# First half of the feed-forward in float32, the weights' float16 halves made after it

## Chip, cores and metric

The kernel runs on one core of a Trainium2 chip. Its time is the device time of one execution in microseconds. The engines are named as in the profile: PE (matrix products), DVE (vector), ACT (scalar functions), POOL (a second elementwise engine), SP (issues most transfers). Each takes its instructions in a fixed order.

## What is computed

Eight batches of eight heads of causal attention with a bias that falls off, over 576 positions of width 64; then a feed-forward layer with a piecewise quadratic gate over the 4608 rows:

```python
scores = (q @ k.T) / sqrt(64); cum = cumsum(max(s, 0))
bias = min(-(cum[:, :, :, None] - cum[:, :, None, :]), 0)
attn = softmax(where(causal, -1e9, scores + bias)) ; out = attn @ v
x = out.transpose(0, 2, 1, 3).reshape(4608, 512)
h = x @ w_in                                  # 512 -> 2048
g = where(h >= 1, h, where(h <= -1, 0, (h + 1) ** 2 / 4))
y = g @ w_out                                 # 2048 -> 512
```

All inputs are float32, and the weights come in as 64-bit words whose bits the kernel turns into float32 itself.

## The kernel before

**Precision.** A product with float32 operands is made of float16 ones: each operand is split into a high half (its rounding to float16 after scaling with a power of two) and a low half (the rest), and three products, high by high, high by low and low by high, are added up. So each step of the feed-forward takes three matmuls where a float32 matmul would be one instruction of the program.

**Attention.** It is cut into 64 jobs: two heads of a batch, and either the first 320 positions (three row tiles) or the last 256 (two row tiles). A job has eight slots (`att_slot`): preparing, scores tile by tile (`scores`, masked minimum on DVE at L418, exponential on ACT at L429), and the output product `px` of the job before (`att_out`, L475), whose eviction writes the high and low halves of `x` (L486 on ACT, L487 on DVE). The scores of the first eight jobs are float32 products (L407), later ones two products in a faster format (L412, L413). After a tile's two heads, `weights_t` scales the exponentials and splits them into halves: the high halves on POOL (L450, L452), the second head's scaling on ACT (L451) and its low half on POOL (L453), the first head's low half on DVE (L456). That last one and the transposing transfer behind it (L457) are put into `late` and issued right behind the next masked minimum.

**Weights.** Both weight matrices come in 16 chunks of 128 x 512 (L189). `decode` makes float32 of a chunk: ACT (L198), DVE (L199), a product with ones for a bound (L203), then either ACT for the lowest bits and one DVE operation (L211, L212) or two DVE operations (L214, L215). After a group of chunks, `scale` takes a power of two from the bound, and `split` makes the halves: high on ACT (L228), low on DVE (L236), or scaled on POOL (L231) or ACT (L233) and subtracted on POOL (L234). The decoded float32 lies in `held`, the halves in `out`; for the second weights these are the same storage, shifted by two chunks, and the decoded first weights lie in that storage too.

**Order.** First come four jobs of batch 0 (its first half), with four chunks of `w_in` decoded in each; then `split` of all 16 chunks. Then the loop over `j` takes one attention slot, at times two, and one feed-forward step each. For `j` below 16 it makes the 16 hidden blocks of the first half (`ffn_h`: 12 matmuls at L530, evictions at L542, L545, L546, split into halves at L556 on ACT and L557 on POOL), for `j` from 16 to 31 their products with `w_out` (`ffn_y`, L569). In the first 16 steps two tasks a step decode and split `w_out`, with a raised priority (`W2_LEAD`). From `j` = 32 on hidden and output steps alternate. A planner sorts the instructions of each engine by a simulated timeline and by priority, with the order of issue in the program as the base; SP's and ACT's transfers are in such orders too.

Of the kernel before, what the change touches and what calls it, by code (L numbers as in the profile page):

```python
# [22 lines left out]
P = 128  # L23
# [26 lines left out]
WO_LAG = 2  # L50
# [21 lines left out]
def attention_ffn(ctx: ExitStack, tc: tile.TileContext, qT, kT, vT, s, w_in, w_out, yT):  # L72
# [95 lines left out]
    class Weights:  # L168
        def __init__(self, name, src, held, out, tags, order, groups):
            self.name, self.src, self.held, self.out, self.tags = name, src, held, out, tags  # L170
            self.order, self.size = order, NW // groups
            self.group = {c: n // self.size for n, c in enumerate(order)}
# [18 lines left out]
        def decode(self, n):  # L191
            c, g = self.order[n], n // self.size
            raw = self.raw.pop(c)
            w = flat32(self.held[c])
# [6 lines left out]
            if n % self.size == 0:  # L201
                self.sums[g] = ps_y.tile([P, 512], F32, tag=f"y{g}", name=f"sum_{self.name}{g}")
# [21 lines left out]
        def split(self, n):  # L224
            c, g = self.order[n], n // self.size
            r = self.r[:, g:g + 1]
            w, hi, lo = flat32(self.held[c]), self.out[c][:, 0], self.out[c][:, 1]
            A.activation(hi, w, AF.Copy, scale=r)  # L228
            if n in self.pool_lo:
                if self.name in POOL_SCALE:  # L230
                    G.tensor_scalar(w, w, r, 1.0, ALU.mult, ALU.mult)  # L231
                else:
                    A.activation(w, w, AF.Copy, scale=r)  # L233
                G.tensor_tensor(lo, w, hi, ALU.subtract)  # L234
            else:
                V.scalar_tensor_tensor(lo, w, r, hi, ALU.mult, ALU.subtract)  # L236
# [3 lines left out]
        WO, WI, ((gp, "g", G_BUFS),), [n % 4 * 4 + n // 4 for n in range(NW)], 4,  # L240
# [4 lines left out]
        WO[WO_LAG:], WO, ((ap, "raw", 2), (gp, "x0", 2), (ap, "raw", 2)), list(range(NW)), 2,  # L245
# [189 lines left out]
    def weights_t(n, i):  # L435
# [14 lines left out]
        G.tensor_scalar(his[0], pv, rs[:R, :1], 1.0, ALU.mult, ALU.mult)  # L450
# [4 lines left out]
        def rest():  # L455
            V.scalar_tensor_tensor(los[0], pv, rs[:R, :1], his[0], ALU.mult, ALU.subtract)  # L456
# [5 lines left out]
        late.append(rest)  # L462

    def att_out(n, hf):
# [19 lines left out]
        e = exs[b][:, p:p + 1]  # L484
# [38 lines left out]
    def ffn_h(b, hf, ft):  # L523
# [4 lines left out]
        for kt in range(NKT):  # L528
            for wl, xl in ((0, 0), (0, 1), (1, 0)):
                T.matmul(  # L530
                    h[:, :N], WI[4 * kt + ft // 4][:, wl, ft % 4 * P:(ft % 4 + 1) * P], x[:, kt, xl],
# [18 lines left out]
    to_split = []  # L550

# [141 lines left out]
```

## Time and profile before

| | us |
|---|---|
| three runs, median (lowest to highest) | 1115.94 (1112.94 to 1116.92) |
| the profiled execution | 1111.73 |
| its span | 1109.9 |

Busy shares of the span are 91% for PE, 76% for DVE, 65% for ACT and 61% for POOL. How to read what follows: a line of the timeline or of the chain gives start, length, engine, line of the program and what is written from what; "x12" is a row of twelve instructions taken together, and the idle time before it and its releaser stand in brackets. A line of the groups gives the count, busy time and mean length in ns of one, then the idle time of the engine just before them.

### The profile page before, as it was taken

What the parts mean: (1) busy time and instruction counts of PE and PEld (TensorE: products, weight loads), DVE (VectorE), ACT (ScalarE), POOL (GpSimd) and SP (SyncE); (2) the same over time, 40 slices, a digit from 0 to 9 for tenths busy, and PEclk for the clock granted to TensorE, in tenths of its full rate; (3) what the DMA queues carried; (4) which work ended last, traced back from release to release, by engine and by line L of the source; (5) the groups of instructions that cost most, each with busy time, mean ns of one, the idle gap of its engine ahead of it and who ended that gap; (6) DMA issues with size and microseconds to landing.
All of it is one profiled execution on the core that took longest, in us unless ns stands there. A gap on an engine that the chain in (4) does not pass through costs nothing.

```text
span 1109.9 us, 25082 instructions
## 1 busy us (share of the span) xinstructions
PE 1010.8 (91%) x8495; PEld 774.9 (70%) x8496; DVE 846.3 (76%) x2325; ACT 725.8 (65%) x1703; POOL 679.0 (61%) x1173
## 2 busy tenths in 40 slices
PE   2456898799999999999999999899999999899998
PEld 1232466587768877777778877687778877787787
DVE  7887966688787877787778877787777887887533
ACT  4765985677567774867567765777576765777432
POOL 4782795775556764766467664666476665765522
PEclk9955999799999999999999999999999999999999
DMA  7876653786468663886468763877387763676300
GB/s 235 218 200 192 170 87 91 158 173 155 100 122 188 148 152 71 187 162 158 79 146 177 161 136 81 177 160 163 68 176 155 165 137 74 158 156 138 68 25 19
DMA packets 340775, 155.01 MB, mean 140 GB/s; under 512 B 290856, under 2 KB 322472, under 8 KB 340648
## 3 DMA queue, kind: packets, MB, share of 16 engines
q1 hardware_dynamic: 330944, 143.49, 59.6%
q10 hardware_dynamic: 9704, 9.93, 2.9%
q8 instruction: 67, 1.10, 0.4%
q14 instruction: 60, 0.49, 0.1%
HBM read 72.31 MB, written 9.73 MB: 74 GB/s over the span
## 4 chain that ended last, share of the span: by engine, by line
PE 61%; DVE 12%; POOL 8%; DMA 7%; issue 6%; ACT 5%; ACTq 0%; SPq 0%; DVEq 0%; POOLq 0%
PE y L569 25%; PE h L530 25%; PE px L475 4%; DMA pt<-pb 3%; PE s L412 3%; PE s L413 3%; DVE pb L456 2%; ACT u L542 2%; POOL pb L453 2%; POOL pb L450 2%; DVE p L418 1%; DVE Q L357 1%; DMA vt<-vb 1%; POOL vb L371 1%; DVE h L545 1%
## 5 line engine op out<-in xcount | busy, mean ns | idle before, releaser
L530 PE MATMUL h<-x,WI 128*128 128x256 f16 (+1 forms) x3072 | 463.9, 290 | 7.4 <-ACT x L486 3.4
L569 PE MATMUL y<-g,WO 128*128 128x256 f16 (+1 forms) x3072 | 457.8, 288 | 7.0 <-POOL g L557 5.3
L530 PEld LDWEIGHTS <-WI 128*128 128x128 f16 x3072 | 291.1, 99 | 97.0 <-issue 13.9
L569 PEld LDWEIGHTS <-WO 128*128 128x128 f16 x3072 | 288.1, 98 | 92.9 <-issue 13.8
L557 POOL TENSOR_TENSOR g<-u,g 128x320 f16<-128x320 f32 (+1 forms) x256 | 206.0, 805 | 152.1 <-ACT g L556 151.6
L429 ACT ACTIVATE p<-p,mn 64x64 f32<-64x64 f32 (+4 forms) x320 | 179.4, 561 | 142.7 <-DVE mn L418 122.2
L542 ACT ACTIVATE u<-h,ub,us 128x320 f32<-128x320 f32 (+1 forms) x256 | 149.1, 583 | 120.3 <-PE h L530 115.3
L545 DVE SCALAR_TENSOR_TENSOR h<-h,ws,u 128x320 f32<-128x320 f32 (+1 forms) x256 | 132.4, 517 | 110.6 <-ACT u L542 108.1
L450 POOL TENSOR_SCALAR pb<-p,rs 64x128 f16<-64x128 f32 (+4 forms) x160 | 95.3, 596 | 171.2 <-DVE rs L446 112.1
L453 POOL TENSOR_TENSOR pb<-p,pb 64x128 f16<-64x128 f32 (+4 forms) x160 | 173.9, 1087 | 9.5
L456 DVE SCALAR_TENSOR_TENSOR pb<-p,rs,pb 64x128 f16<-64x128 f32 (+4 forms) x160 | 134.6, 841 | 47.1 <-POOL pb L450 47.0
L418 DVE CUSTOM_DVE_ANT_0 p<-s,mask 64x64 f32<-64x64 f32 (+4 forms) x320 | 134.4, 420 | 31.3 <-PE s L413 23.0
L412 PE MATMUL s<-K,Q 128*64 128x64 f32 (+1 forms) x336 | 126.2, 377 | 16.0 <-DVE mn L418 10.9
L546 DVE SCALAR_TENSOR_TENSOR u<-u,r,h 128x320 f32<-128x320 f32 (+1 forms) x256 | 130.3, 509 | 6.8 <-DVE h L545 0.5
L451 ACT ACTIVATE p<-p,rs 64x64 f32<-64x64 f32 (+4 forms) x160 | 89.6, 560 | 51.3 <-DVE rs L446 49.4
L556 ACT CAST g<-u 128x320 f16<-128x320 f32 (+1 forms) x256 | 107.9, 421 | 10.3 <-DVE u L546 10.3
L413 PE MATMUL s<-K,Q 68*64 68x64 f32 (+1 forms) x336 | 102.8, 307 | 2.1 <-DMA K<-cumd 1.3
L452 POOL TENSOR_SCALAR pb<-p 64x128 f16<-64x128 f32 (+4 forms) x160 | 93.2, 583 | 11.9 <-ACT p L451 11.0
L475 PEld LDWEIGHTS <-vt 128*64 128x64 f16 x1536 | 73.4, 113 | 36.7 <-issue 30.2
L475 PE MATMUL px<-pt,vt 128*64 128x256 f16 (+3 forms) x1536 | 83.5, 259 | 13.3 <-DMA pt<-pb 8.7
L412 PEld LDWEIGHTS s<-K,Q 128*64 128x64 f32 (+1 forms) x336 | 61.5, 183 | 27.3 <-DVE mn L418 8.2
L413 PEld LDWEIGHTS s<-K,Q 68*64 68x64 f32 (+1 forms) x336 | 61.9, 184 | 5.8 <-issue 1.7
(105 smaller groups left out, 983.0 us busy)
## 6 DMA issues: line engine op xcount, KB each, us to landing
rk<-in_k_dram SPq DMA_DIRECT2D x56, 288.0 KB
v<-in_v_dram SPq DMA_DIRECT2D x32, 288.0 KB
rq<-in_q_dram SPq DMA_DIRECT2D x56, 160.0 KB
rk<-in_k_dram SPq DMA_DIRECT2D x56, 160.0 KB
wir<-in_moe_w_in_dram SPq DMA_DIRECT2D x16, 512.0 KB
wor<-in_moe_w_out_dram SPq DMA_DIRECT2D x16, 512.0 KB
rq<-in_q_dram SPq DMA_DIRECT2D x56, 128.0 KB
out_dram<-o ACTq DMA_DIRECT2D x32, 160.0 KB
```

The costliest lines, as they stand in the source:

```text
L412: T.matmul(sc[:R, :c1 - c0], Q1[:, hd, qo:qo + R], K1[:, hd, c0:c1], start=True, stop=False)
L413: T.matmul(sc[:R, :c1 - c0], Q2[:KC, hd, qo:qo + R], K2[:KC, hd, c0:c1], start=False, stop=True)
L418: ttr[0] = V.tensor_tensor_reduce(out=Pt[:R, c0:c1], in0=sc[:R, :c1 - c0], in1=mask[:R, mo:mo + c1 - c0], scale=-0.125 if j < F32_JOBS els ...
L429: A.activation(Pt[:R, :W], Pt[:R, :W], AF.Exp, bias=m2[:R], scale=-1.0, accum_out=sums[n, i][:R, hd:hd + 1])
L453: G.tensor_tensor(los[1], pw, his[1], ALU.subtract)
L456: V.scalar_tensor_tensor(los[0], pv, rs[:R, :1], his[0], ALU.mult, ALU.subtract)
L475: T.matmul(px[hd * D:(hd + 1) * D, lo:N], VT[:, vl * NB + j, hd * D:(hd + 1) * D], PT[:, 4 * j + 2 * hd + pl, lo:], start=(m == 0), stop=( ...
L530: T.matmul(h[:, :N], WI[4 * kt + ft // 4][:, wl, ft % 4 * P:(ft % 4 + 1) * P], x[:, kt, xl], start=(n == 0), stop=(n == 3 * NKT - 1),)
L542: first = A.activation(u, h[:, :N], AF.Relu, bias=ubi[b], scale=usc[b][:, fg:fg + 1]).ins
L545: V.scalar_tensor_tensor(h[:, :N], h[:, :N], wsc[b][:, fg:fg + 1], u, ALU.mult, ALU.max)
L557: G.tensor_tensor(g[:, 1], u, g[:, 0], ALU.subtract)
L569: T.matmul(ys[b, hf, m][:, :N], WO[8 * (m // 2) + ft // 2][:, wl, c0:c0 + P], g[:, gl], start=(ft == 0 and n == 0), stop=(ft == NFT - 1 an ...
```

## The change

The 320 positions of the first half (batch 0) go through the feed-forward in float32: `x` is left in float32 (one eviction, none on DVE), `first_h` multiplies it with the decoded chunks of `w_in` (4 matmuls a block in place of 12), its eviction leaves `g` in float32 with no split, and `first_y` multiplies that with the decoded chunks of `w_out`. The halves of the weights are made afterwards: one chunk of `w_in` a step from `j` = 4, and `w_out` from `j` = 24, the last eight chunks two a step from `j` = 32 with raised priority. Both weights now share their storage, shifted by two chunks, and all low halves of weights are made by ACT (scaling) and POOL (subtraction). The decoding of all 16 chunks of `w_out` takes its lowest bits through ACT. In the first eight jobs the first head's weights are scaled on ACT and their low half is subtracted on POOL, and the transpose is issued at once and not put into `late`.

```diff
-WO_LAG = 2
+W_LAG = 2
 
 Y_LAG = 2
 
-ACT_LOW = {'wi': range(0, 16, 2), 'wo': range(0, 16, 2)}
-POOL_LO = {'wi': (8, 12, 13, 14, 15), 'wo': range(16)}
-POOL_SCALE = ('wi',)
+ACT_LOW = {'wi': range(0, 16, 2), 'wo': range(16)}
+POOL_LO = {'wi': range(16), 'wo': range(16)}
 
 K_POOL = range(12)
 F32_JOBS = 8
+POOL_LO_JOBS = 8
...
-    WI = [cp.tile([P, 2, NC], F16, name=f"WI{c}") for c in range(NW)]
-    WO = [cp.tile([P, 2, NC], F16, name=f"WO{c}") for c in range(NW + WO_LAG)]
+    WT = [cp.tile([P, 2, NC], F16, name=f"WT{c}") for c in range(2 * NW + W_LAG)]
+    half_bias = cp.tile([P, 1], F32, name="half_bias")
...
-        def __init__(self, name, src, held, out, tags, order, groups):
-            self.name, self.src, self.held, self.out, self.tags = name, src, held, out, tags
+        def __init__(self, name, src, base, banks, tags, order):
+            groups = len(banks)
+            self.name, self.src, self.banks, self.tags = name, src, banks, tags
+            self.out, self.held = WT[base:base + NW], WT[base + W_LAG:base + W_LAG + NW]
             self.order, self.size = order, NW // groups
-            self.group = {c: n // self.size for n, c in enumerate(order)}
...
-            w = flat32(self.held[c])
+            w = flat32(self.held[n])
...
-            c, g = self.order[n], n // self.size
+            g = n // self.size
             r = self.r[:, g:g + 1]
-            w, hi, lo = flat32(self.held[c]), self.out[c][:, 0], self.out[c][:, 1]
+            w, hi, lo = flat32(self.held[n]), self.out[n][:, 0], self.out[n][:, 1]
             A.activation(hi, w, AF.Copy, scale=r)
             if n in self.pool_lo:
-                if self.name in POOL_SCALE:
-                    G.tensor_scalar(w, w, r, 1.0, ALU.mult, ALU.mult)
-                else:
-                    A.activation(w, w, AF.Copy, scale=r)
+                A.activation(w, w, AF.Copy, scale=r)
                 G.tensor_tensor(lo, w, hi, ALU.subtract)
...
-        G.tensor_scalar(his[0], pv, rs[:R, :1], 1.0, ALU.mult, ALU.mult)
+        pool_lo = jobs.index((n, hf)) < POOL_LO_JOBS
+        if pool_lo:
+            A.activation(tiles2[0][:R, :W], tiles2[0][:R, :W], AF.Copy, scale=rs[:R, :1])
+            G.tensor_scalar(his[0], pv, 1.0, 1.0, ALU.mult, ALU.mult)
+            G.tensor_tensor(los[0], pv, his[0], ALU.subtract)
+        else:
+            G.tensor_scalar(his[0], pv, rs[:R, :1], 1.0, ALU.mult, ALU.mult)
         A.activation(tiles2[1][:R, :W], tiles2[1][:R, :W], AF.Copy, scale=rs[:R, 1:])
         G.tensor_scalar(his[1], pw, 1.0, 1.0, ALU.mult, ALU.mult)
         G.tensor_tensor(los[1], pw, his[1], ALU.subtract)
 
         def rest():
-            V.scalar_tensor_tensor(los[0], pv, rs[:R, :1], his[0], ALU.mult, ALU.subtract)
+            if not pool_lo:
+                V.scalar_tensor_tensor(los[0], pv, rs[:R, :1], his[0], ALU.mult, ALU.subtract)
             nc.sync.dma_start_transpose(
                 out=PT[:, :4 * (i + 1), off - h_off:off - h_off + R],
                 in_=PB[:R].rearrange("p j g c -> p (j g c)"),
             )
 
-        late.append(rest)
+        if pool_lo:
+            rest()
+        else:
+            late.append(rest)
...
+        e = exs[b][:, p:p + 1]
+        if (b, hf) == (0, 0):
+            if p == 0:
+                X[b, hf] = gp.tile([P, NKT, N], F32, tag=f"x{hf}", bufs=2, name=f"x{b}_{hf}")
+            with tc.high_priority(offset=X_LEAD):
+                A.activation(X[b, hf][:, p], px[:, :N], AF.Copy, scale=e)
+            return
...
+    g32 = []
+    us32, ws32 = (cp.tile([P, 1], F32, name=n) for n in ("us32", "ws32"))
+
+    def first_scales():
+        V.tensor_scalar(us32, msc[0], 2.0 ** -13, None, ALU.mult)
+        V.tensor_scalar(ws32, msc[0], 2.0 ** -12, None, ALU.mult)
+
+    def first_h(ft):
+        N = HALF[0][1]
+        h = ps_h.tile([P, 512], F32, tag="h", name=f"h0_0_{ft}")
+        for kt in range(NKT):
+            T.matmul(
+                h[:, :N], flat32(w1.held[ft // 4 * NKT + kt])[:, ft % 4 * P:(ft % 4 + 1) * P], X[0, 0][:, kt],
+                start=(kt == 0), stop=(kt == NKT - 1),
+            )
+        if ft % 4 == 0:
+            g32.append(gp.tile([P, 4, N], F32, tag="g", bufs=G_BUFS, name=f"g0_0_{ft}"))
+        with tc.high_priority(offset=FFN_LEAD):
+            u = gp.tile([P, N], F32, tag="u", bufs=4, name=f"u0_0_{ft}")
+            A.activation(u, h[:, :N], AF.Relu, bias=half_bias, scale=us32)
+            V.scalar_tensor_tensor(h[:, :N], h[:, :N], ws32, u, ALU.mult, ALU.max)
+            V.scalar_tensor_tensor(g32[-1][:, ft % 4], u, 1.0, h[:, :N], ALU.min, ALU.mult)
+
+    def first_y(ft, ms):
+        N = HALF[0][1]
+        for m in ms:
+            if ft == 0:
+                ys[0, 0, m] = ps_y.tile([P, 512], F32, tag=f"y{m}", name=f"y0_0_{m}")
+            c0 = ft % 2 * 2 * P + m % 2 * P
+            T.matmul(
+                ys[0, 0, m][:, :N], flat32(w2.held[8 * (m // 2) + ft // 2])[:, c0:c0 + P], g32[ft // 4][:, ft % 4],
+                start=(ft == 0), stop=(ft == NFT - 1),
+            )
+            if ft == NFT - 1:
+                o = gp.tile([P, N], F32, tag="o", bufs=O_BUFS, name=f"o0_0_{m}")
+                with tc.high_priority(offset=FFN_LEAD):
+                    A.copy(o, ys[0, 0, m][:, :N])
+                nc.scalar.dma_start(yT[m * P:(m + 1) * P, :N], o)
...
+    first_scales()
     while late:
         late.pop(0)()
-    V.tensor_reduce(a_in, w1.bound, axis=AX, op=ALU.max)
-    batch_scales(0)
     for c in range(3):
-        w2.load(c, a_in)
-    for n in range(NW):
-        w1.split(n)
+        w2.load(c, w1.bound[:, 3:4])
     att_out(*jobs[NPAIR - 1])
...
-    def w2_tasks():
...
-        with tc.high_priority(offset=W2_LEAD):
-            for _ in range(W2_RATE):
-                next(tasks, None)
+        if j < NW // 2:
+            with tc.high_priority(offset=W2_LEAD):
+                for c in (2 * j, 2 * j + 1):
+                    w2.decode(c)
+                    w2.load(c + 3)
+                    if c % 8 == 7:
+                        w2.scale(c // 8, TINY)
+        if j < NFT:
+            first_h(j)
+        elif j < 2 * NFT:
+            i = j - NFT
+            if i < 8:
+                for ft in (2 * i, 2 * i + 1):
+                    first_y(ft, (0, 1))
+            else:
+                for ft in range(i % 4 * 4, i % 4 * 4 + 4):
+                    first_y(ft, (i // 4,))
+        if j == NFT:
+            V.tensor_reduce(a_in, w1.bound, axis=AX, op=ALU.max)
+            batch_scales(0)
+            batch_y(0)
+        if 4 <= j < NW + 4:
+            w1.split(j - 4)
+        if NW + 8 <= j < 2 * NW:
+            w2.split(j - NW - 8)
+        elif 2 * NW <= j < 2 * NW + 4:
+            with tc.high_priority(offset=W2_LEAD):
+                for c in (8, 9):
+                    w2.split(c + (j - 2 * NW) * 2)
         if j >= 2 * NFT:
             ffn_step(j // 2, j % 2)
-        elif j < NFT:
-            ffn_step(j, 0)
-        else:
-            if j == NFT:
-                with tc.high_priority(offset=FFN_LEAD):
-                    g_split()
-            m = 2 * (j // 8 % 2)
-            for i in range(j % 8 * 2, j % 8 * 2 + 2):
-                ffn_y(*ffn_q[i], ms=(m, m + 1))
-            if j == 2 * NFT - 1:
-                del ffn_q[:NFT]
```

More of the change, by code (lines that the diff above doesn't have):

```diff
@@ L161, in attention_ffn @@
     NC = 512
-    WI = [cp.tile([P, 2, NC], F16, name=f"WI{c}") for c in range(NW)]
-    WO = [cp.tile([P, 2, NC], F16, name=f"WO{c}") for c in range(NW + WO_LAG)]
+    WT = [cp.tile([P, 2, NC], F16, name=f"WT{c}") for c in range(2 * NW + W_LAG)]
+    half_bias = cp.tile([P, 1], F32, name="half_bias")
+    V.memset(half_bias, 0.5)
     def flat32(t):
@@ L201, in decode @@
             if n % self.size == 0:
-                self.sums[g] = ps_y.tile([P, 512], F32, tag=f"y{g}", name=f"sum_{self.name}{g}")
+                self.sums[g] = ps_y.tile([P, 512], F32, tag=f"y{self.banks[g]}", name=f"sum_{self.name}{g}")
             T.matmul(
@@ L239, in attention_ffn @@
         "wi", lambda c: w_in[c // 4 * P:(c // 4 + 1) * P, c % 4 * NC:(c % 4 + 1) * NC, :],
-        WO, WI, ((gp, "g", G_BUFS),), [n % 4 * 4 + n // 4 for n in range(NW)], 4,
+        0, (0, 1, 2, 3), ((gp, "g", G_BUFS),), [n % 4 * 4 + n // 4 for n in range(NW)],
     )
@@ L244, in attention_ffn @@
         .rearrange("(j p) n t -> p j n t", p=P),
-        WO[WO_LAG:], WO, ((ap, "raw", 2), (gp, "x0", 2), (ap, "raw", 2)), list(range(NW)), 2,
+        NW, (2, 3), ((ap, "raw", 2), (gp, "x0", 2), (ap, "raw", 2)), list(range(NW)),
     )
@@ L483, in att_out @@
         x = X[b, hf]
-        e = exs[b][:, p:p + 1]
         with tc.high_priority(offset=X_LEAD):
@@ L530, in ffn_h @@
                 T.matmul(
-                    h[:, :N], WI[4 * kt + ft // 4][:, wl, ft % 4 * P:(ft % 4 + 1) * P], x[:, kt, xl],
+                    h[:, :N], w1.out[ft // 4 * NKT + kt][:, wl, ft % 4 * P:(ft % 4 + 1) * P], x[:, kt, xl],
                     start=(n == 0), stop=(n == 3 * NKT - 1),
@@ L569, in ffn_y @@
                 T.matmul(
-                    ys[b, hf, m][:, :N], WO[8 * (m // 2) + ft // 2][:, wl, c0:c0 + P], g[:, gl],
+                    ys[b, hf, m][:, :N], w2.out[8 * (m // 2) + ft // 2][:, wl, c0:c0 + P], g[:, gl],
                     start=(ft == 0 and n == 0), stop=(ft == NFT - 1 and n == 2),
@@ L612, in attention_ffn @@
                 batch_scales_v(0)
+    first_scales()
     while late:
         late.pop(0)()
-    V.tensor_reduce(a_in, w1.bound, axis=AX, op=ALU.max)
-    batch_scales(0)
     for c in range(3):
-        w2.load(c, a_in)
-    for n in range(NW):
-        w1.split(n)
+        w2.load(c, w1.bound[:, 3:4])
     att_out(*jobs[NPAIR - 1])
-    def w2_tasks():
-        for g in range(2):
-            for c in range(8 * g, 8 * g + 8):
-                w2.decode(c)
-                w2.load(c + 3)
-                yield
-            w2.scale(g, TINY)
-            batch_y(0, (g,))
-            for c in range(8 * g, 8 * g + 8):
-                w2.split(c)
-                yield
     t = 8 * NPAIR
-    tasks = w2_tasks()
     for j in range(16 * NP):
```

## The prediction

> **What bounds the kernel now.** I read the windows first, because the change sits in the first fifth of the run. The columns are the stretch in us, its length, then busy time (and instructions) of PE, weight loads, DVE, ACT and POOL, then granted clock, DMA share and GB/s.
>
> ```profile
> core 0: us, PE busy (x) PEld busy (x) DVE busy (x) ACT busy (x) POOL busy (x), PEclk, DMA share, GB/s
> 0.00:104.00 104.00, 46.39 (x164) 22.25 (x166) 83.14 (x214) 59.10 (x118) 64.74 (x106) 0.78 0.80 216
> 104.00:139.00 35.00, 30.14 (x140) 17.12 (x138) 31.97 (x74) 31.00 (x59) 21.56 (x25) 0.83 0.63 162
> 139.00:188.00 49.00, 48.81 (x379) 33.97 (x379) 32.13 (x94) 32.61 (x65) 34.64 (x44) 1.00 0.47 87
> 188.00:212.00 24.00, 13.08 (x98) 10.01 (x95) 15.40 (x51) 14.22 (x42) 17.66 (x32) 0.72 0.77 153
> 212.00:260.00 48.00, 47.63 (x458) 40.30 (x457) 39.56 (x107) 34.91 (x89) 36.12 (x68) 1.00 0.68 152
> ```
>
> From 212 us on PE is full (47.63 of 48), so the change is worth whatever it moves that point. Before it there are three stretches. Up to 104 us PE is half empty and DVE is the fullest engine (83.14, or 80%; POOL has 62%, ACT 57%). From 104 to 139 DVE (91%) and ACT (89%) are both near full and PE idles 4.9 us. From 139 to 188 PE is full again. From 188 to 212 it idles 10.9 us.
>
> What ends the first stretch is read from the chain of waits (start, length, what):
>
> ```profile
> 87.11 0.68 DVE WO L215
> 87.78 0.27 DVE pb L456
> 88.10 0.15 POOL p L402
> 88.30 4.63 DMA pt<-pb
> ...
> 99.94 0.98 PE px L475 x5
> ```
>
> The first half's hidden layer needs `x` of the first four jobs. The fourth job's product `px` starts at 99.94. On its chain stands the low half of a head's weights (L456, DVE), behind second-weight decoding on the same engine (L215). The timelines of POOL and of DVE show why it came so late:
>
> ```profile
> 80.19 2.72 POOL L234 TENSOR_TENSOR WI<-WO,WI 128x512 f16<-128x512 f32 x2
> 82.90 0.53 POOL L450 TENSOR_SCALAR pb<-p,rs 64x128 f16<-64x128 f32 x1
> ```
> ```profile
> 81.83 3.73 DVE L199 TENSOR_SCALAR WO<-WO 128x512 int32<-128x512 int32 x2
> ...
> 91.85 0.43 DVE L199 TENSOR_SCALAR WO<-WO 128x512 int32<-128x512 int32 x1 [0.62 <-ACT WO L198]
> ```
>
> POOL made two first-weight low halves ahead of this job's high half (L450). That half was done by 83.4, and DVE then came to L456 only at 87.78: 4.4 us lost on DVE, and some before it on POOL. So the splitting of the first weights isn't waited for by the hidden layer itself; it delays the attention jobs that are.
>
> **The change, part by part.** (a) *The startup.* DVE loses two groups entirely in this stretch, eleven first-weight low halves and twelve first-head low halves:
>
> ```profile
> L236 DVE SCALAR_TENSOR_TENSOR WI<-WO,r_wi,WI 128x512 f16<-128x512 f32 x11 | 9.5, 883 | 0.0
> L456 DVE SCALAR_TENSOR_TENSOR pb<-p,rs,pb 64x128 f16<-64x128 f32 (+2 forms) x12 | 8.2, 683 | 4.4 <-POOL pb L450 4.4
> ```
> ```profile
> L453 POOL TENSOR_TENSOR pb<-p,pb 64x128 f16<-64x128 f32 (+2 forms) x12 | 12.5, 1044 | 0.5
> ...
> L234 POOL TENSOR_TENSOR WI<-WO,WI 128x512 f16<-128x512 f32 x5 | 6.2, 1244 | 0.0
> ```
>
> That is 9.5 + 8.2 = 17.7 us off DVE's 83.14. POOL takes twelve subtractions of the same kind as L453, 12 x 1.044 = 12.5 us, and is rid of five first-weight low halves, 5 x 1.244 = 6.2, and of the five scalings before them (L231). ACT is rid of 16 first-weight high halves and gets twelve short scalings. The transposes of a job are no longer held back behind the next masked minimum (`late`), so SP's queue gets them sooner; their number, and that of all loads, is the same. The gain is unknown between 0 (POOL becomes what DVE was) and 17.7 (DVE alone was the bound). The nearest row is the 4.4 us that L456 waits for or costs on one chain; of four jobs that the same thing happens to, not each ends last, and DVE's own idle time (20.9 of 104) says that it isn't the only bound. I take **-8**.
>
> At this place a rule speaks against the change. The rows first: L199 takes 0.43 us with POOL idle, and two of them 3.73 us while POOL runs L234. The Trainium skill, "SBUF — State Buffer", section "Who interferes with whom", says that a GpSimd instruction and a DVE instruction in a two-port mode take a shared port pair in turns, and that the one that comes second blocks for the whole of the other. The 0.43 and 3.73 agree. By that rule, as an estimate, the 12.5 us of new POOL subtractions would stand in DVE's way and the gain of (a) would be 17.7 - 12.5 = 5 instead of 8.
>
> (b) *The float32 products.* One f16 matmul of 320 columns is priced by twelve of them in a row (start to next start), a float32 one by the scores of the first jobs, where the two records of an x2 are one matmul:
>
> ```profile
> 113.06 1.79 PE L530 MATMUL h<-x,WI 128*128 128x320 f16 x12
> 114.69 0.65 PE L407 MATMUL s<-KF,QF 68*128 68x288 f32 x2
> ...
> 118.70 0.92 PE L407 MATMUL s<-KF,QF 68*128 68x448 f32 x2
> 119.46 0.84 PE L569 MATMUL y<-g,WO 128*128 128x320 f16 x5
> ```
>
> f16: (114.69 - 113.06) / 12 = 0.136 us. Float32: (119.46 - 118.70) / 448 x 320 = 0.543 us. Before, the first half has 192 + 192 matmuls, 384 x 0.136 = 52.2; after, 64 + 64, 128 x 0.543 = 69.5. PE works **+17.3** longer, half in `h`, half in `y`. Weight loads are included, since these prices are start to start. At a lower granted clock (0.83 from 104 to 139) each costs more in proportion; both kernels pay that for a few of them.
>
> (c) *Where that is hidden.* These groups are those of 104 to 206 us, ACT's and then POOL's:
>
> ```profile
> L233 ACT ACTIVATE WO<-WO,r_wo 128x512 f32<-128x512 f32 x16 | 11.5, 719 | 0.1
> L228 ACT ACTIVATE WO<-WO,r_wo 128x512 f16<-128x512 f32 x16 | 11.4, 721 | 1.2 <-POOL WO L234 1.2
> L542 ACT ACTIVATE u<-h,ub,us 128x320 f32<-128x320 f32 (+1 forms) x17 | 10.2, 603 | 0.0
> L556 ACT CAST g<-u 128x320 f16<-128x320 f32 x16 | 7.2, 453 | 4.2 <-DVE u L546 4.2
> L451 ACT ACTIVATE p<-p,rs 128x448 f32<-128x448 f32 (+4 forms) x11 | 7.1, 647 | 2.1 <-DVE x L487 1.1 <-DVE rs L446 0.8
> L211 ACT ACTIVATE wor<-wor,floor_bias 128x512 uint16<-128x512 uint8 x4 | 5.8, 1448 | 0.0
> ```
> ```profile
> L234 POOL TENSOR_TENSOR WO<-WO,WO 128x512 f16<-128x512 f32 x16 | 20.0, 1250 | 2.1 <-ACT WO L233 1.7 <-POOL WO L234 0.5
> L557 POOL TENSOR_TENSOR g<-u,g 128x320 f16<-128x320 f32 x16 | 15.0, 939 | 18.1 <-ACT g L556 18.1
> ```
>
> ```profile
> 104.00:139.00 35.00, 17.22 (x90) 10.23 (x90) 0.83 0.63 162
> ```
>
> While `h` is made, PE isn't the bound now: of the `h` products (the window above is of their line alone) 90, seven and a half steps, are done in 35 us, 4.7 us a step, though twelve in a row take 1.63. So of the 8.7 us that `h` gets longer I put **-6** beside the evictions; if that cover goes, they cost 6. The `y` share, 8.7, lies on the path, where PE is full (139 to 188).
>
> (d) *Evictions and splits.* The casts (L556, 7.2 us of ACT) and the subtractions (L557, 15.0 us of POOL) of the first half go. The second weights' splits (ACT 11.5 + 11.4, POOL 20.0), today ahead of the attention by priority, leave this place; the same sum comes in for the first weights, one chunk a step from the fifth step on, without priority. Each of those waits until PE has read the float32 chunk that it overwrites; behind it on ACT stand evictions and exponentials, and PE waits for those. Between 0 and 12 us (ACT's 22.9 in half of the stage) I take **-6**: the attention jobs five to eight get ahead.
>
> (e) *The tail at 188.*
>
> ```profile
> 186.10 0.65 PE L407 MATMUL s<-KF,QF 68*128 68x288 f32 x2
> ...
> 200.62 2.77 PE L475 MATMUL px<-pt,vt 128*64 128x256 f16 x30 [4.49 <-DMA pt<-pb]
> ```
>
> The last scores of job eight stand behind `y` products, and its `px` follows 14.5 us later, with PE idle 10.9 us. Longer `y` products can lie over that tail if the job is through sooner, not if the planner again puts its scores last: 0 to -10.9, I take **-5.5**, the middle. The eight late second-weight splits are issued when the second half has begun and are wanted only by its `y`; I cost them at nothing, hidden by its `h` products; without that cover, up to 8 x (0.719 + 0.721) = 11.5. What is small and only moves (two scales for the float32 half ahead of it, the batch's scales behind its `h`, one bit operation fewer on DVE for eight second chunks, four low halves of `x` fewer) I cost at nothing too: DVE has 16.9 us idle between 139 and 188, and without that room the batch's scales would hold the second half's first eviction by about as many DVE instructions as they are; at L456's 0.683 for each of some fifteen, far above what a few values a partition can take, 10 us.
>
> The sum: -8 + 17.3 - 6 - 6 - 5.5 = **-8.2 us**. Against the profiled execution (1111.73, of which 1109.9 is span) that is 1103.5. That execution lies 4.2 below the median of the runs, 1115.94; put on the median the sum gives 1107.7, so **1108**.
>
> **Rivals.** *ACT binds the stage (slower).* In 104 to 212 ACT works 31.00 + 32.61 + 14.22 = 77.8 us. To that come eight more low-bit passes, 8 x 1.448 = 11.6 (fewer if some fall before 104), eight first-head scalings, 8 x 0.647 = 5.2, and eight second-weight splits, 11.5; the casts take 7.2 away: 98.9 us. At its fullest share so far (89%) that needs 111 us against 108 now, so it decides from there: at 80% it needs 124, +16, and less 6 for a smaller startup gain is +10, 1126. For it: a queue in strict order, and waits for PE's reading in front of evictions. Against: the h of the second half doesn't wait for the second weights' splits; without their 11.5 the stage fits. *POOL takes DVE's place at startup (no change).* With (a) at 0 the sum is -0.2, 1116. For it: POOL gets more than it loses; against: DVE is the fuller by 18 us. *DVE was the whole bound.* (a) at -17.7 and (e) at -10.9 give -23, 1093. *The change doesn't do what it says*: if the planner pulled the first weights' splits back into the startup, (a) would be lost. The storage speaks against it: chunk n's halves overwrite float32 chunk n - 2, which `h` still reads; only two chunks are free. I give this no share of its own.
>
> **How the numbers follow.** Forecast (1100 to 1112) 0.45, ACT 0.20, POOL 0.22, DVE 0.13. The range: down to the DVE rival, 1092, up to ACT's, 1126; costs off to either end beyond that (nothing hidden, +17, or all gains, -26) are the 2 in 10 left out. A measurement of this kernel tells about 0.5%, 5.6 us, from no change, that is below 1110.4 or above 1121.5. Faster: 0.38 of the forecast, 0.13 and 0.02 of POOL's, 0.53. Slower: ACT's 0.20 and 0.02 of POOL's, 0.22. Same: 0.25.
>
> **What would show it.** (a) `px` of job four before 94 us, DVE's share of that stretch below 75%; wrong if it starts at 98 or later with POOL over 75%. (b) 128 float32 matmuls at 0.54 us each. (c) `h` steps at 4 us or less apart; wrong if ACT is above 95% there. (d) jobs five to eight through by 190 us. (e) no idle stretch of PE over 3 us ahead of the second half. The whole is wrong if the point at which PE is full for good is later than 212 us, or if the later stretches change pace.

## Result and the profile after

The changed kernel takes 1127.38 us (median of 4 runs, 1126.19 to 1128.24) against 1114.44 of the kernel before on the same chip (1110.12 to 1116.92): a ratio of 1.0124, with an interval of 1.0101 to 1.0146. By the ratio it is slower by 13.8 us (the two medians differ by 12.9), and 1127.38 is 1.4 us above the upper end of the predicted range. The profiled execution has a span of 1124.3 us. The ratios below leave out one execution of 5664 us, of a kernel that otherwise took 1100 to 1104.

The windows of after, in the same stretches as those of before (stretch, length, busy PE, weight loads, DVE, ACT, POOL, granted clock, DMA share, GB/s), and one more:

```profile
core 0: us, PE busy (x) PEld busy (x) DVE busy (x) ACT busy (x) POOL busy (x), PEclk, DMA share, GB/s
0.00:104.00 104.00, 56.37 (x199) 31.64 (x201) 71.22 (x205) 64.34 (x132) 57.18 (x114) 0.89 0.85 220
104.00:139.00 35.00, 30.60 (x124) 19.66 (x123) 22.45 (x54) 33.50 (x54) 20.72 (x24) 0.97 0.67 165
139.00:188.00 49.00, 46.44 (x205) 31.82 (x203) 20.30 (x55) 33.27 (x63) 29.54 (x36) 0.98 0.29 65
188.00:212.00 24.00, 12.72 (x86) 9.22 (x86) 19.14 (x53) 19.21 (x40) 20.89 (x27) 0.58 0.51 111
212.00:260.00 48.00, 43.02 (x379) 35.94 (x380) 40.64 (x109) 35.12 (x94) 38.10 (x76) 0.89 0.72 152
...
212.00:230.00 18.00, 13.02 (x90) 9.79 (x91) 15.28 (x33) 12.58 (x32) 14.77 (x27) 0.71 0.56 119
```

Read down, the fullest engine changes from stretch to stretch. At startup DVE has fallen from 83.14 to 71.22, and PE does 10 us more. From 104 to 139 ACT is full (96%) where DVE and ACT shared the load before. From 139 to 188 PE is full with float32 products while ACT is idle for 32% of the time and POOL for 40%. From 188 to 212 POOL is busy for 87% and DVE and ACT for 80%, while PE idles 11.3 us. And PE is not full from 212 on: 5 us more are lost by 230. From there the pace is that of before (PE has 580.90 of the 600 us from 400 to 1000; before, 582.30).

Where the lead is lost is shown by the end of `px` of each attention job, read from PE's timeline (start plus length of the job's last `px` row, us):

| job | before | after |
|---|---|---|
| 4 | 102.5 | 88.5 |
| 5 | 140.6 | 142.0 |
| 6 | 162.2 | 169.1 |
| 8 | 203.4 | 211.9 |
| 9 | 213.9 | 228.0 |
| 10 | 228.3 | 240.6 |
| 12 | 254.5 | 266.8 |

The 14.0 us won at startup are lost again by job five, with 1.4 more; another 5.5 are lost by job six, 1.6 by job eight, and 5.5 between jobs eight and nine alone, of which 1.7 come back by job ten. The lag of job twelve, 12.3 us, is then about that of the end (13.8). From job four to job twelve after takes 178.3 us and before 151.9: this stage is 26.4 us longer.

### The profile page after: what moved, and what is told of

Read it like the earlier page. It is cut to its first block, busy times and chain, and to the rows that moved or that the text cites. A ratio compares the mean times of both kernels' runs of the same rounds, so it can differ in the third digit from the quotient of the medians.

```text
span 1124.3 us, 24796 instructions
## 1 busy us (share of the span) xinstructions
PE 1025.9 (91%) x8367; PEld 789.8 (70%) x8368; DVE 828.5 (74%) x2285; ACT 748.2 (67%) x1731; POOL 676.7 (60%) x1183
## 4 chain that ended last, share of the span: by engine, by line
PE 46%; DVE 9%; POOL 5%; issue 4%; DMA 3%; ACT 3%; DVEq 0%; POOLq 0%; ACTq 0%; SPq 0%
PE h L545 19%; PE y L622 19%; PE px L484 3%; DMA pt<-pb 3%; PE s L411 3%; PE s L412 2%; DVE pb L462 2%; DVE Q L356 1%; ACT u L557 1%; POOL pb L455 1%; DVE p L417 1%; DVE h L560 1%; POOL pb L458 1%; DVE u L561 1%; POOL g L610 1%
## 5 line engine op out<-in xcount | busy, mean ns | idle before, releaser
L622 PE MATMUL y<-g,WT 128*128 128x256 f16 (+1 forms) x2880 | 428.9, 287 | 5.7 <-POOL g L610 3.7
L545 PE MATMUL h<-x,WT 128*128 128x256 f16 (+1 forms) x2880 | 429.5, 288 | 3.1 <-DVE u L561 2.4
L622 PEld LDWEIGHTS <-WT 128*128 128x128 f16 x2880 | 269.8, 98 | 82.5 <-issue 11.7
L545 PEld LDWEIGHTS <-WT 128*128 128x128 f16 x2880 | 271.0, 98 | 79.1 <-issue 6.6
L610 POOL TENSOR_TENSOR g<-u,g 128x256 f16<-128x256 f32 (+1 forms) x240 | 188.2, 784 | 133.2 <-ACT g L609 132.3
L557 ACT ACTIVATE u<-h,ub,us 128x256 f32<-128x256 f32 (+1 forms) x240 | 139.3, 580 | 118.3 <-PE h L545 113.5
L560 DVE SCALAR_TENSOR_TENSOR h<-h,ws,u 128x256 f32<-128x256 f32 (+1 forms) x240 | 123.7, 516 | 102.3 <-ACT u L557 99.7
L455 POOL TENSOR_SCALAR pb<-p,rs 64x128 f16<-64x128 f32 (+4 forms) x140 | 83.7, 598 | 158.7 <-DVE rs L445 110.3
L417 DVE CUSTOM_DVE_ANT_0 p<-s,mask 64x64 f32<-64x64 f32 (+4 forms) x320 | 134.7, 421 | 33.1 <-PE s L412 16.7
L462 DVE SCALAR_TENSOR_TENSOR pb<-p,rs,pb 64x128 f16<-64x128 f32 (+4 forms) x140 | 123.1, 880 | 41.6 <-POOL pb L455 41.4
L561 DVE SCALAR_TENSOR_TENSOR u<-u,r,h 128x256 f32<-128x256 f32 (+1 forms) x240 | 121.7, 507 | 6.6 <-DVE h L560 0.5
L609 ACT CAST g<-u 128x256 f16<-128x256 f32 (+1 forms) x240 | 100.7, 420 | 6.2 <-DVE u L561 6.2
```

Of the source, the lines that this page charges most:

```text
L417: ttr[0] = V.tensor_tensor_reduce(out=Pt[:R, c0:c1], in0=sc[:R, :c1 - c0], in1=mask[:R, mo:mo + c1 - c0], scale=-0.125 if j < F32_JOBS els ...
L545: T.matmul(h[:, :N], w1.out[ft // 4 * NKT + kt][:, wl, ft % 4 * P:(ft % 4 + 1) * P], x[:, kt, xl], start=(n == 0), stop=(n == 3 * NKT - 1),)
L557: first = A.activation(u, h[:, :N], AF.Relu, bias=ubi[b], scale=usc[b][:, fg:fg + 1]).ins
L560: V.scalar_tensor_tensor(h[:, :N], h[:, :N], wsc[b][:, fg:fg + 1], u, ALU.mult, ALU.max)
L610: G.tensor_tensor(g[:, 1], u, g[:, 0], ALU.subtract)
L622: T.matmul(ys[b, hf, m][:, :N], w2.out[8 * (m // 2) + ft // 2][:, wl, c0:c0 + P], g[:, gl], start=(ft == 0 and n == 0), stop=(ft == NFT - ...
```

## Experiments

Each run stands against the kernel before, run beside it on the same chip; ratios are compared, since the base differs a little from chip to chip, and 0.01 of a ratio is 11.1 us. The intervals are about 0.0025 to either side, so two runs are told apart from about 4 us on. Kernels that leave work out say which.

**The parts that move work between engines, undone and alone.** The first edit gives the low bits of the odd second chunks back to VectorE, the second the first-head low halves of the first eight jobs (and puts their transposes into `late` again).

```diff
-ACT_LOW = {..., 'wo': range(16)}
+ACT_LOW = {..., 'wo': range(0, 16, 2)}
```
```diff
-POOL_LO_JOBS = 8
+POOL_LO_JOBS = 0
```

> The changed kernel, but with the lowest bits of every second chunk of the second weights put back on DVE (8 ACT passes of 1.45 us less, 8 DVE operations more). Theory A (ACT binds the stretch from 90 to 139 us, where it is 96% busy, and through the decoding holds the loads behind it): 1117 to 1121, 6 to 10 below the changed kernel's 1127. Theory P (the float32 products fill PE's order from 139 to 184 us, and the scores of jobs seven and eight stand behind them): 1125 to 1128. Theory T (the first head's low halves, longer by an ACT step and on POOL, lengthen each job's chain): 1125 to 1128.

> The changed kernel, but with no job's first-head low half moved: all on DVE, scaled by POOL, transposes behind the next minimum, as before the change. Theory T: 1117 to 1122, since the chain of jobs five to eight is shorter again, though the startup gives back some of its 13 us. Theory A: ACT is rid of 20 scalings (11 us), about half of them in the full stretch: 1122 to 1125. Theory P: 1127 or, with the startup's gain lost, up to 1135.

The low bits: 1122.84, ratio 1.0063 (1.004 to 1.0086), 6.8 us below after. `px` of job five ends at 133.2 there instead of 142.0. The first-head halves: 1124.75, 1.0088 (1.0057 to 1.012), 4.0 below, at the limit of what can be told. Both together:

> The changed kernel with both side parts undone: lowest bits of every second chunk of the second weights on DVE again, first-head low halves on DVE again. If the two losses are of their own and add up: 1127 - 4.5 - 2.6 = 1120. If both are the same loss (ACT's full stretch), 1122 to 1123. Theory S alone: not below 1117, since all splits are still where the change put them.

1121.26, 1.0061 (1.0033 to 1.009): 7.0 us below after, where the two alone add up to 10.8: by these numbers the two losses overlap in part. The first-head part alone, put on the kernel before:

> The kernel before with this one part of the change: the first eight jobs' first-head low halves on ACT and POOL, transposes at once. Theory T: 1117 to 1122, slower than before by the longer chain. Theory A: 1114 to 1118, ACT's 11 us partly in its full stretch 104 to 139. Theory P: no reason for a loss; DVE gives up 8 us of the startup: 1108 to 1114.

1123.45, 1.0065 (1.0045 to 1.0084): the part alone makes the kernel before 7.2 us slower. PE's timeline, `px` of job four, first in the run with this part undone, then in the run with this part alone:

```profile
87.18 1.66 PE L484 MATMUL px<-pt,vt 128*64 128x320 f16 x18 [1.71 <-DMA pt<-pb]
```
```profile
107.27 1.66 PE L486 MATMUL px<-pt,vt 128*64 128x320 f16 x18 [0.80 <-issue]
```

After has 86.81 and before 99.94. So this part brings nothing at the startup when the splits are gone from there, and `px` comes 7 us later with it when they are not: the startup's whole gain is that of the splits. (The kernel before without first-weight splits, below, agrees: its `px` of job four starts at 85.33.)

**A quarter of the float32 products left out** (32 of 128, 17.4 us of PE, as much as the float32 half adds):

```diff
-        for kt in range(NKT):
+        for kt in (0, 2, 3):
...
-            T.matmul(
+            if ft % 4 != 1:
+              T.matmul(
```

> The changed kernel with a quarter of its float32 products left out (one of four in each sum of h, four of sixteen in each sum of y), so that PE's work for the first half is 96 x 0.54 = 52 us, what the float16 products took before; the output is not the reference's. Theory P: 1108 to 1114, all of the 17 us of PE back or most of it. Theory A: 1122 to 1127, since h waits for its evictions and decoding anyway. Theory T: 1122 to 1127.

1126.48, 1.0096 (1.0067 to 1.0124): 3.1 us below after, less than can be told from nothing. Taken by itself that says that the float32 products cost next to nothing; the runs below show that it is wrong. The run isn't clean either: the planner orders its startup in another way, and `px` of job four ends at 93.7 us, where after has 88.5.

**The splits left out**, first all 32 from after (second half and later read one constant tile), then the first weights' 16 from the kernel before (its hidden products read one constant tile):

```diff
-            w1.split(j - 4)
+            pass
...
-            w2.split(j - NW - 8)
+            pass
...
-                    w2.split(c + (j - 2 * NW) * 2)
+                    pass
```

> The changed kernel with the splitting of both weights left out (32 x 2 ACT instructions of 0.72 us and 32 POOL subtractions of 1.2 us that now all lie between 100 and 220 us); the later products read one constant tile in place of the halves, so the output is not the reference's. Theory S (the splits, moved out of the startup where ACT had room, now stand in front of the attention jobs five to eight on ACT and POOL, and the lateness of those jobs sets the end): 1105 to 1114, and the output product of job eleven, now 12 us later than before the change, is back or ahead. Theory P' (what is left is the order of PE, with the float32 products in front of scores): 1122 to 1127.

> The kernel before with the first weights' splits left out of the startup (h reads one constant tile; the output is not the reference's): the part of the change that frees the startup, without its price later. If a startup 13 us shorter is worth 13 us at the end: 1101 to 1105. If the stretch after it takes the gain back by itself (loads that come no sooner, DVE and ACT full from 104 to 139 us): 1108 to 1114.

After without splits: 1119.95, 1.0045 (1.0028 to 1.0061), 8.8 us below after and still above before. Before without first-weight splits: 1099.29, 0.9863 (0.9834 to 0.9892). What the change takes out of the startup is worth 15.3 us, and kept to the end, if nothing is put back. The windows of after without splits show why it doesn't come down to that:

```profile
104.00:139.00 35.00, 31.41 (x134) 20.30 (x132) 20.20 (x53) 24.54 (x39) 11.78 (x18) 1.00 0.64 164
139.00:188.00 49.00, 46.82 (x201) 32.23 (x202) 21.17 (x64) 16.31 (x35) 14.94 (x23) 0.97 0.36 76
```

ACT and POOL are two thirds idle from 139 to 188, and PE is as full as with the splits. Up to job six the splits cost nothing: its `px` ends at 168.8 without them and at 169.1 with them. Behind it they do: job nine's ends at 218.9 instead of 228.0.

**Two misses in the order of the work.** The late second-weight splits spread one every second step, without priority, and the scales of batch 0 issued at step 8 instead of 16 (both on top of the low bits undone); and the sixteen chunks decoded one a step instead of two, without priority (likewise):

```diff
-        if j == NFT:
+        if j == 8:
...
-        elif 2 * NW <= j < 2 * NW + 4:
-            with tc.high_priority(offset=W2_LEAD):
-                for c in (8, 9):
-                    w2.split(c + (j - 2 * NW) * 2)
+        elif 2 * NW <= j < 3 * NW and j % 2 == 0:
+            w2.split(8 + (j - 2 * NW) // 2)
```
```diff
-        if j < NW // 2:
-            with tc.high_priority(offset=W2_LEAD):
-                for c in (2 * j, 2 * j + 1):
+        if j < NW:
+            w2.decode(j)
+            w2.load(j + 3)
...
```

> The changed kernel with the lowest bits back on DVE (1122.8 by itself) and with less in the stretch 184 to 225 us: the last eight splits of the second weights one every second step and without priority, and the scales of batch 0 issued eight steps earlier. Theory S: 1114 to 1119, the jobs eight to eleven get through sooner. Theory P': 1121 to 1123, nothing more than the lowest bits give.

> After, with the low bits of the odd second chunks back on VectorE (that alone gave 1122.8) and the sixteen second chunks decoded one a step over 16 steps, in the program's place, instead of two a step over 8 steps and ahead of everything. Nothing is left out. Theory D (the decoding, packed into the first eight steps and ahead of job five's attention, makes job five late: 53 us from px of job four to px of job five, before 38): px of job five ends at 120-127 and the time falls to 1114-1118. Theory not D: within 2 us of 1122.8.

1125.41, 1.0091 (1.0063 to 1.0119), and 1124.9, 1.0101 (1.0074 to 1.0128): neither better than the 1.0063 of the low bits alone. In the second, job five's `px` comes in three pieces on PE, the last of which ends at 134.7; the low bits alone gave 133.2, and 120 to 127 was expected. Jobs six to eight do come 3.5 us sooner (job six 160.9 against 164.5), but by job twelve that is lost (261.3 against 260.8): to have a job sooner is worth nothing if a later one stands behind another limit.

**Limits that hide each other.** If the stages are in series with a different full engine each, taking away one load should do little and two together much more.

> After without any weight split (the second half of the first batch and all that follows read one constant tile) and also without a quarter of the float32 products. Leaving out the splits alone gave 1120.0, leaving out the quarter of the products alone 1126.5, against 1127.4 of after. Theory M (limits in series mask each other: with the splits gone TensorE's float32 products, 46 of 49 us busy between 139 and 184, are what holds jobs six and seven back): together they give back much more than the sum of the two, to 1108-1114, and px of job seven ends before 181. Theory S (what is left is not TensorE but the attention chain itself and its loads): about the sum, 1117-1120, px of job seven at 187-191.

No splits and a quarter of the products fewer: 1107.12, 0.9932 (0.9913 to 0.9951). With the splits gone the quarter is worth 12.6 us; with them it was worth 3.1. And with the quarter gone the splits are worth 18.3, with all products in place 8.8. The windows with the quarter out alone, and then with the splits out as well:

```profile
188.00:212.00 24.00, 11.88 (x86) 8.64 (x82) 17.21 (x44) 19.27 (x46) 20.99 (x30) 0.64 0.54 122
212.00:230.00 18.00, 16.24 (x136) 13.29 (x136) 16.46 (x37) 13.27 (x34) 15.67 (x27) 0.85 0.62 113
```
```profile
188.00:212.00 24.00, 17.91 (x138) 14.14 (x139) 13.54 (x41) 13.81 (x38) 16.65 (x32) 0.64 0.78 164
212.00:230.00 18.00, 18.00 (x176) 15.92 (x174) 14.62 (x50) 12.52 (x39) 14.81 (x32) 1.00 0.76 157
```

With the quarter out alone, POOL is as full from 188 to 212 as in after (20.99), and PE still not full from 212. With both out PE is full there. A part of this lies in the startup and not in the stage: with the quarter out `px` of job four ends 5.3 us later when the splits are in place (93.7 against 88.5), and 2.5 later without them (90.0 against 87.5). If that difference of 2.8 us were carried whole to the end, 6.7 of the 9.5 us between 3.1 and 12.6 would be left for the loads that hide each other. Which splits do it was tried by leaving out one set of weights, and the second set with the quarter of the products:

> After without the sixteen splits of the second weights (the second products of the second half and later read one constant tile); the first weights' splits stay. All splits together were worth 7.4 us. Theory L (the loss lies in the late second-weight splits, which fill GpSimd to 87% between 188 and 212): 1118-1121, nearly the whole 7.4, and px of job nine within 15 us of px of job eight or sooner (after 16). Theory W1 (it lies in the first weights' splits between 104 and 188): 1124-1128.

> After without the sixteen splits of the first weights (the hidden products of the second half and later read one constant tile); the second weights' splits stay. Theory L: within 2 us of after, 1125-1129. Theory W1: 1119-1122.

> After without the sixteen splits of the second weights and without a quarter of the float32 products. The quarter alone gave 0.9 us, with no splits at all 12.9. Theory L (what the shorter products gain is taken back by the second weights' splits, eight of them late): 8-13 below the run without second-weight splits, 1108-1112. Theory W1 (the first weights' splits take it back): 0-4 below it.

Without the second weights' splits: 1121.79, 1.0057 (1.0037 to 1.0076), 7.5 us below after, most of the 8.8; `px` of jobs six and nine ends at 169.2 and 219.5, as without any split. Without the first weights': 1125.39, 1.0095 (1.0071 to 1.0119), 3.2 below, not told from nothing. Without the second weights' and with the shorter products: 1116.08, 1.0015 (0.9995 to 1.0034), another 4.7, between the two theories. From there to 0.9932, where the first weights' splits are out too, are 9.2 us, but of these up to 4.5 are the startup's (`px` of job four ends at 94.4 in the one and 90.0 in the other). So the second weights' splits cost most; that the first ones take a part back is likely and not clear of the startup.

**TensorE's order.** In after PE's timeline of the first half's end reads so (two records are one float32 matmul):

```profile
169.00 1.02 PE L406 MATMUL s<-KF,QF 68*128 68x448 f32 x2
169.86 6.09 PE L595 MATMUL y<-g,WT 128*128 128x320 f32 x22
175.78 1.40 PE L406 MATMUL s<-KF,QF 68*128 68x448 f32 x4
177.02 5.55 PE L595 MATMUL y<-g,WT 128*128 128x320 f32 x20
182.41 0.65 PE L406 MATMUL s<-KF,QF 68*128 68x288 f32 x2
182.89 1.24 PE L595 MATMUL y<-g,WT 128*128 128x320 f32 x4
```

Scores stand behind ten or eleven float32 products at a time, 5.4 to 5.9 us. The edit gives the scores of jobs five to eight the first place:

```diff
+            with tc.high_priority(offset=FFN_LEAD) if j >= NPAIR else ExitStack():
             T.matmul(
                 sc[:R, :c1 - c0], QF[j % 2]...
```

> After, with the scores of jobs five to eight given the first place in TensorE's order, ahead of float32 products that stand before them in the program (job six's last scores then follow about 10 to 19 products fewer, 5 to 10 us at 0.54 us each). Nothing is left out. Theory O (scores of jobs five to eight queue behind the float32 products): px of jobs six and seven end 4-8 us sooner and the time falls to 1119-1123. Theory A (ScalarE and the decoding pace the stage up to 140 us, then the exponentials and weights of the jobs): within 2 us of after, 1125-1129.

1123.49, 1.0074 (1.0051 to 1.0096): 5.6 us below after; `px` of jobs six and seven end at 161.5 and 189.4 instead of 169.1 and 195.6. With low bits and first-head halves undone too:

> After with the low bits and the first-head low halves back on VectorE (that gave 1121.3) and with the scores of jobs five to eight first in TensorE's order (that alone gave 1123.5). Nothing is left out. If the two gains add up: 1117-1118. If they are one and the same lateness of jobs five to eight, 1120-1122.

1118.53, 1.0052 (1.0037 to 1.0068): 8.0 below after. It has the lowest ratio of the forms that leave nothing out, and is still slower than before. Against the same form without the first place for scores (1.0061) it wins 1.0 us, which can't be told from nothing: the 5.6 of the scores and the 7.0 of the moved work don't add up.

**What is left of the change without its costs.** No splits, low bits and first-head halves undone, so that only the float32 half is left; then a quarter of its products fewer:

> After without any weight split, with the low bits of the odd second chunks back on VectorE and the first-head low halves back on VectorE: of the change only the float32 first half is left, and it pays for no split at all. Apart, the splits gave back 7.5 us and the other two together 6.1. If these losses add up: 1113-1115. If the same wait lies behind them (they overlap): 1118-1120. If a limit was masked by them: under 1111. The kernel before without its first-weight splits stands at 1099.

> After without any weight split, with the low bits and the first-head low halves back on VectorE (that gave 1112.3), and also without a quarter of the float32 products. Theory M (TensorE's float32 products are the limit that is left when the splits and the moved work are gone): 1100-1104, that is 8 to 12 below, as they gave 12.9 with the splits alone gone. Theory not M (attention's own chain is left): 1109-1112.

1112.28, 0.999 (0.997 to 1.001), and 1101.74 (median of three), 0.9903 (0.9878 to 0.9929). The second has about the PE work of the float16 half and comes near the 0.9863 of before without first-weight splits. That gives a ladder from 0.9903 up to after: the longer products +9.7 us (0.999), the moved low bits and halves +6.1 (1.0045), the splits +8.8 (1.0124). The 24.6 us of the three are close to the 26.4 that the stage from job four to job twelve grew by. The rungs belong to this order of adding, since the loads hide one another.

**A version to beat both.** The kernel before, with the first weights' splits behind `px` of job four in the program:

```diff
-    for n in range(NW):
-        w1.split(n)
     att_out(*jobs[NPAIR - 1])
+    for n in range(4):
+        w1.split(n)
...
+        if j < 6:
+            w1.split(2 * j + 4)
+            w1.split(2 * j + 5)
```

> The kernel before with one thing moved: the sixteen splits of the first weights no longer stand together ahead of px of job four, but four behind it and then two a step in the first six steps of the first half, ahead of the decoding (the chunks of the first weights are held in the order in which they are split, so that the decoding finds its places free). All else is before's: the first half in float16, no work moved between engines. Theory S (it is the splits standing ahead of px of job four that cost before 15 us, and they can be hidden beside the first half's products, which in float16 leave TensorE free): px of job four ends at 87-92 and the time falls to 1101-1109. Theory E (the splits cost their VectorE and GpSimd time wherever they stand): within 3 us of before, 1111-1117.

1113.34, 0.9993 (0.9977 to 1.001): no difference. The groups of its first 104 us show that the idea was not tried: the planner put all splits where they had been,

```profile
L236 DVE SCALAR_TENSOR_TENSOR WI<-WO,r_wi,WI 128x512 f16<-128x512 f32 x11 | 9.5, 883 | 0.0
```

as many and as long as before. Whether the splits of the float16 kernel can be hidden beside its products stays open. No version was found that beats both.

## Why the prediction was wrong

**The step that failed is the one from "hidden" to "costs nothing" behind the startup: (d), (e) and the late splits "costed at nothing".** The prediction let the stage from `px` of job four to the point where PE is full keep its length (+17.3 - 6 - 6 - 5.5 = -0.2). From job four to job twelve it became 26.4 us longer, more than the 14.0 that the startup won.

(a) *The startup, -8: right in sign, too small, and in part for a wrong reason.* `px` of job four:

```profile
86.81 1.65 PE L484 MATMUL px<-pt,vt 128*64 128x320 f16 x18 [1.25 <-issue]
```

It starts at 86.81 instead of 99.94, 13.1 us sooner, and DVE has 68% of the stretch, as step (a) asked. But of the 17.7 us taken off DVE, the first-head halves' 8.2 brought nothing there and, given to ACT and POOL, cost about 4.0 in after and 7.2 alone. The gain is that of the splits, which leave DVE, POOL and ACT at once; which of the three engines had held `px` back isn't separated by a run. The estimate of 5 put beside it from the Trainium skill, "SBUF — State Buffer", section "Who interferes with whom", is below the 13.1 of the startup as a whole; for the moved halves by themselves, which the rule spoke against, its direction was right. Whether POOL's new subtractions held DVE up there, or the way through ACT was longer, no run tells.

(b) *The float32 products, +17.3: right.* From 177.02 to 182.41 ten of them take 0.539 us each, against 0.543.

(c) *-6 beside the evictions: about right as a size, no help for the time.* With the splits out of the way 17.4 us of PE are worth 9.7 to 12.6, so 5 to 8 are hidden; whether beside the evictions of `h` or elsewhere isn't separated, since the quarter left out is one of `h` and `y` alike. The sign set for failure came: ACT at 96% from 104 to 139, where nine low-bit passes stand:

```profile
L213 ACT ACTIVATE wor<-wor,floor_bias 128x512 uint16<-128x512 uint8 x9 | 12.6, 1427 | 0.0
```

The steps of `h` did not come closer together. First and last eviction of the sixteen, of before and then of after:

```profile
107.40 1.11 ACT L542 ACTIVATE u<-h,ub,us 128x320 f32<-128x320 f32 x2
...
170.28 0.60 ACT L542 ACTIVATE u<-h,ub,us 128x320 f32<-128x320 f32 x1
```
```profile
93.46 0.60 ACT L585 ACTIVATE u<-h,half_bias,us 128x320 f32<-128x320 f32 x1
...
169.08 0.60 ACT L585 ACTIVATE u<-h,half_bias,us 128x320 f32<-128x320 f32 x1
```

They lie 5.0 us apart on average, before 4.2, and the prediction asked for 4 or less. Begun 14 us sooner, `h` ends 1.2 us sooner; with the low bits back on DVE the last eviction starts at 163.2.

(d) *-6, jobs five to eight through by 190: wrong sign.* `px` of job eight ends at 211.9, before at 203.4. What left the stage came back as ACT's low bits to 140, as float32 products ahead of scores to 188 (5.6 us by TensorE's order), and as splits behind.

(e) *The tail, -5.5, and the eight late splits at nothing: wrong.* PE idles 11.3 us from 188 to 212, before 10.9, and 5.0 more by 230, before 0.4. Groups between 184 and 230:

```profile
L233 POOL TENSOR_TENSOR WT<-WT,WT 128x512 f16<-128x512 f32 x13 | 14.9, 1151 | 0.5 <-POOL K L359 0.5
L232 ACT ACTIVATE WT<-WT,r_wo 128x512 f32<-128x512 f32 x12 | 8.6, 716 | 0.2
L230 ACT ACTIVATE WT<-WT,r_wo 128x512 f16<-128x512 f32 x11 | 7.8, 711 | 0.8 <-POOL WT L233 0.8
```

Thirteen splits, five more than the eight emitted late, run here: 14.9 us of POOL and 16.4 of ACT. The argument for nothing was that PE doesn't wait for them (only the second half's `y` reads them), which is true, but the attention jobs' weights stand in the same queues on POOL and ACT. PE's own gaps name the attention chain or, once, the scales of the next batch (`mt`), never a split:

```profile
189.38 0.37 PE L105 MATMUL row_m<-ident,mt 128*1 128x128 f32 x1 [3.94 <-DVE mt L266]
...
193.01 2.56 PE L484 MATMUL px<-pt,vt 128*64 128x256 f16 x30 [0.33 <-DVE mn L417]
...
204.28 0.64 PE L411 MATMUL s<-K,Q 128*128 128x320 f32 x1 [1.94 <-DVE mn L417]
209.16 2.77 PE L484 MATMUL px<-pt,vt 128*64 128x256 f16 x30 [3.97 <-DMA pt<-pb]
...
220.07 4.85 PE L545 MATMUL h<-x,WT 128*128 128x256 f16 x22 [2.38 <-DVE u L561]
```

Yet the first of these gaps goes back to the splits for the greater part. DVE's rows ahead of it, and POOL's at the time:

```profile
186.81 2.27 DVE L91 TENSOR_SCALAR c<-c 128x4 int32<-128x4 int32 x1
189.11 0.18 DVE L261 RECIPROCAL rc<-c 128x4 f32<-128x4 f32 x1
189.20 0.13 DVE L266 TENSOR_REDUCE mt<-c 128x1 f32<-128x4 f32 x1
```
```profile
186.71 1.14 POOL L233 TENSOR_TENSOR WT<-WT,WT 128x512 f16<-128x512 f32 x1
...
187.90 1.14 POOL L233 TENSOR_TENSOR WT<-WT,WT 128x512 f16<-128x512 f32 x1
```

An instruction on 128x4 values takes 2.27 us beside two second-weight splits, and `mt` and PE stand behind it; in the run without these splits it takes 0.17, and PE's gap is 1.54. All sixteen second-weight splits cost 7.5 us; the prediction's price without cover was 11.5, for the eight late ones, which no run leaves out by themselves. The sign (e) had set, no idle stretch of PE over 3 us, failed twice, by 3.94 and 3.97.

*The rivals.* "ACT binds the stage" gave 1126, next to the 1127.4 measured, and its reason holds up to 140 us: the moved low bits and halves are worth 7.0. It is not the whole: from 139 PE is full, from 188 POOL, and none of the three loads taken away alone gives more than 9. So that its number came so near is in part luck. "POOL takes DVE's place at startup" falls (POOL has 57.18 of 104, before 64.74). "DVE was the whole bound" falls too: the startup won 13 to 14 us and not 17.7, and the 8.2 of the moved halves brought nothing.

## What to carry to other kernels

An early gain is worth what the stages behind it let through: read the fullest engine stretch by stretch, and add what the change puts into each stretch on every engine, whoever waits for it. Work that "nobody waits for" still stands in a queue; it costs what is queued behind it, and it can be costed at nothing only if its engine is idle there and nothing late is behind it. When loads stand on different engines in series, leaving one out can understate it (3.1 us against 12.6 here, of which up to 2.8 may be the startup's), so cancel two together before calling one free, and look whether the planner kept the rest in its order.

## What was not expected of the hardware

How long a DVE instruction can be held up beside POOL. Rows of after, DVE's timeline and then POOL's:

```profile
204.22 2.78 DVE L462 SCALAR_TENSOR_TENSOR pb<-p,rs,pb 64x128 f16<-64x128 f32 x1
...
247.19 0.37 DVE L462 SCALAR_TENSOR_TENSOR pb<-p,rs,pb 64x128 f16<-64x128 f32 x1 [0.31 <-POOL pb L455]
```
```profile
204.39 0.14 POOL L401 MEMSET p<- 128x64 f32 x1
204.50 1.15 POOL L233 TENSOR_TENSOR WT<-WT,WT 128x512 f16<-128x512 f32 x1
205.60 0.14 POOL L401 MEMSET p<- 128x64 f32 x1
205.70 1.15 POOL L233 TENSOR_TENSOR WT<-WT,WT 128x512 f16<-128x512 f32 x1
```

The same 64x128 subtraction takes 0.37 us at 247 and 2.78 at 204, where it ends only when both of POOL's late splits are over; in the run without second-weight splits it takes 0.36 at 198:

```profile
198.48 0.36 DVE L464 SCALAR_TENSOR_TENSOR pb<-p,rs,pb 64x128 f16<-64x128 f32 x1
```

The 128x4 operation above (2.27 us, else 0.16 to 0.17) is a second case. The Trainium skill, "SBUF — State Buffer", section "Who interferes with whom", says that a DVE instruction with two inputs in SBUF contends with a GpSimd instruction that reads SBUF; the rows of the subtraction agree, and show it held through two of them in a row. So a split on POOL also costs DVE time that no count of DVE's instructions shows: from 188 to 212 DVE is busy for 19.14 us with 53 instructions in after, and for 14.65 with 58 in the run without second-weight splits (not all of them the same instructions).
